# Half-height out matmuls beside the scores, and two gate groups ahead of their value groups

## The chip, the cores and the metric

The kernel runs on one core of a Trainium2 chip. The time is that of the device, in microseconds (us), from start to end of one execution. A time of a kernel is the median of several executions; the profile is of one execution. The engines of the core work from queues of their own: TensorE (PE in the profile, with its weight loads as PEld), VectorE (DVE), ScalarE (ACT), GpSimd (POOL) and the SyncE queue (SP), which here only issues DMAs.

## The reference

Causal attention with 16 extra keys and values ("beacons") that every query may see, for 8 batches of 8 heads with 576 tokens and a head size of 64. Its output, 4608 tokens of 512, goes through a gated feed-forward block with 1536 hidden units.

```
k_all = concatenate([beacon_k, k]);  v_all = concatenate([beacon_v, v])
a = softmax(mask(q @ k_all.T / 8))          # per batch and head
x = (a @ v_all) as 4608 tokens x 512
out = (gelu(x @ w_gate) * (x @ w_val)) @ w_out
```

## The kernel before

One core does everything, batch by batch, and two kinds of work are interleaved: the attention of batch b, and the out projection of chunk b - 1 (a chunk is 512 tokens; there are nine). All engine orders are written out by hand: `keep` holds each instruction in program order on its engine.

**Attention of a batch** (in the loop over `b`). Heads go in four pairs m. The scores of a pair, keys by queries, come in four chunks c of 512, 464, 496 and 208 columns (`CHUNKS`, in the order 0, 2, 1, 3). "Score (m, c)" below is one call part of `scores(b, (m, c))`. Since a head has 64 dimensions, a score matmul uses 64 of the 128 rows of the array; the two heads of a pair use the upper and the lower 64 rows and write to two banks of one buffer. `scores` then has ScalarE take the exp into SBUF (L171), and GpSimd clear the causal triangle (`masks`, L320). `attend` multiplies by the values (`x_ps`), VectorE normalizes (`r_sb`, `y_sb`), and a DMA transpose brings the result to `xT_sb`.

**The feed-forward block of a chunk.** `gate_val(ci, fi)` makes hidden tile fi of twelve: four gate matmuls, four value matmuls (128 rows, 512 columns each), gelu on ScalarE (`ge_sb`), and their product on VectorE (L448, `hT_sb`). `out_mms` makes the out projection, in four token groups ti of twelve matmuls each, summed over fi in one bank, which `out_store` copies to SBUF on VectorE (L467). `o(n)` issues the next n of these 48 matmuls. They lie between the score groups, so that TensorE has work while ScalarE takes exps.

**PSUM.** There are three buffers of two banks (`psum_s`, tag "s"), taken in turn by score groups, by gate/value groups, by some attends and by the transposes of batch 1's last head pair; and two single banks, `psum_t` ("bank t") and `psum_o` ("bank o"), each a pool of one buffer, for out groups (even ti in t, odd ti in o), single-head attends, and transposes. A tile in a pool waits until the readers of the tile that had the buffer before are done.

**The end of a chunk and the start of a batch, before.** Gate/value group 10 takes an "s" buffer. Group 11 is split (`split=True`): its gate goes to bank t, its value to an "s" buffer, so that gelu runs while the value is computed. Then, in batch b, ScalarE loads the table of exp (L593), and TensorE goes: three out matmuls, scores (0,0), (0,2), (0,1), ten out matmuls, scores (0,3)+(1,3), (1,0), (1,2), five out matmuls, the attend of head 0 in bank t, one out matmul, scores (1,1), (2,0), (2,2), the attend of head 1, seven out matmuls, scores (2,1), (2,3)+(3,3), (3,0), and so on. I call the first three score groups the first triple, the next three the second. In batch 1 four transposes of head pair 3 (`transpose_pe`) stand among the ten out matmuls. In chunk 0, the transposes of batch 1's first three head pairs (`transpose_wide`) follow gate/value groups 4, 6 and 8; keys go through bank t and are copied out by VectorE in five copies (L218, L222), queries through bank o and are copied by ScalarE.

Of the kernel before, what the change touches and what calls it, by code (L numbers as in the profile page):

```python
# [7 lines left out]
P = 128  # L8
B, H, S, NB, D = 8, 8, 576, 16, 64
SK = S + NB  # L10
N_TOK = B * S
D_MODEL = 512
D_FF = 1536
F_TILES = D_FF // P
K_CHUNKS = D_MODEL // P
CH = 512
# [24 lines left out]
FP32 = mybir.dt.float32  # L41
BF16 = mybir.dt.bfloat16
ACT = mybir.ActivationFunctionType
ALU = mybir.AluOpType
# [5 lines left out]
def kernel(  # L50
# [12 lines left out]
    nc = tc.nc  # L63
    keep = tc.keep_in_program_order
# [6 lines left out]
    fpool = ctx.enter_context(tc.tile_pool(name="fpool", bufs=3))  # L71
    hpool = ctx.enter_context(tc.tile_pool(name="hpool", bufs=2))
    opool = ctx.enter_context(tc.tile_pool(name="opool", bufs=2))
    psum_s = ctx.enter_context(tc.tile_pool(name="psum_s", bufs=3, space=bass.MemoryType.PSUM))
    psum_t = ctx.enter_context(tc.tile_pool(name="psum_t", bufs=1, space=bass.MemoryType.PSUM))
    psum_o = ctx.enter_context(tc.tile_pool(name="psum_o", bufs=1, space=bass.MemoryType.PSUM))
# [6 lines left out]
    wg_sb = const.tile([P, K_CHUNKS, D_FF], BF16, name="wg_sb", tag="wg_sb")  # L83
    wv_sb = const.tile([P, K_CHUNKS, D_FF], BF16, name="wv_sb", tag="wv_sb")
    wo_sb = const.tile([P, F_TILES, D_MODEL], BF16, name="wo_sb", tag="wo_sb")
    xT_sb = const.tile([P, NPAIR, N_TOK + P - KROWS[4]], BF16, name="xT_sb", tag="xT_sb")
# [80 lines left out]
    def mm(out_ap, lhsT, rhs, start, stop, **kw):  # L167
        keep(nc.tensor.matmul(out_ap, lhsT, rhs, start=start, stop=stop, **kw))  # L168

    def act(out_ap, in_ap, func, **kw):  # L170
        keep(nc.scalar.activation(out_ap, in_ap, func, **kw))  # L171
# [6 lines left out]
    def tr_part(b, m, w, dst):  # L178
        qk, kb = qk6[b]
        for r in range(6):  # L180
            for hi in range(2):
                tr(
                    dst[64 * hi : 64 * hi + 64, r * 96 : (r + 1) * 96],
                    qk[0:96, w, 2 * m + hi, r * D : (r + 1) * D],
                )
        if w:
            tr(dst[:, S:SK], kb[:, 2 * m : 2 * m + 2, :])

    def transpose_pe(b, m, by_act=False):
        t_ps = psum_s.tile([P, 2, 1024], BF16, name="t_ps", tag="s")  # L190
        for w in range(2):
            tr_part(b, m, w, t_ps[:, w, :])
        out_ap = qkT[:, m, :, NB:SK].rearrange("p w (t r) -> p w t r", r=6)
        in_ap = t_ps[:, 0:2, 0:S].rearrange("p w (r t) -> p w t r", r=6)
        keep(nc.vector.tensor_copy(out_ap[:, 1], in_ap[:, 1]))
        if by_act:
            act(out_ap[:, 0], in_ap[:, 0], ACT.Copy)
        else:
            keep(nc.vector.tensor_copy(out_ap[:, 0], in_ap[:, 0]))
        keep(nc.vector.tensor_copy(qkT[:, m, 1, 0:NB], t_ps[:, 1, S:SK]))  # L200
# [208 lines left out]
    h_of, o_of = {}, {}  # L409

    gv_of = {}

    def gv_mms(ci, fi, *kks, split=False, last=False):
        if (ci, fi) not in gv_of:
            if split:
                gv_of[ci, fi] = (
                    psum_t.tile([P, CH], FP32, name="g_ps", tag="t"),
                    psum_s.tile([P, 2, CH], FP32, name="v_ps", tag="s")[:, 0, :],
                )
            else:  # L420
                gv_ps = psum_s.tile([P, 2, CH], FP32, name="gv_ps", tag="s")
                gv_of[ci, fi] = (gv_ps[:, 0, :], gv_ps[:, 1, :])
        n0 = ci * CH

        def part(w):
            for kk in kks:
                mm(
                    gv_of[ci, fi][w],
                    (wg_sb, wv_sb)[w][:, kk, fi * P : (fi + 1) * P],
                    xT_sb[:, kk, n0 : n0 + CH],  # L430
                    kk == 0,
                    last and kk == kks[-1],
                    skip_group_check=True,
                )

        part(0)
        if not split:
            part(1)
        if not last:
            return  # L440
        ge_sb = fpool.tile([P, CH], BF16, name="ge_sb", tag="ge_sb")
        act(ge_sb, gv_of[ci, fi][0], ACT.Gelu)
        if split:
            part(1)
        if ci not in h_of:
            h_of[ci] = hpool.tile([P, F_TILES, CH], BF16, name="hT_sb", tag="hT_sb")
        keep(
            nc.vector.tensor_tensor(  # L448
                out=h_of[ci][:, fi, :], in0=gv_of.pop((ci, fi))[1], in1=ge_sb, op=ALU.mult
            )  # L450
        )

    def gate_val(ci, fi, split=False):
        gv_mms(ci, fi, *range(K_CHUNKS), split=split, last=True)

    def out_mm(ci, ti, fi, o_ps, c0=0, c1=D_MODEL):
        mm(
            o_ps,
            h_of[ci][:, fi, ti * P : (ti + 1) * P],
            wo_sb[:, fi, c0:c1],  # L460
            fi == 0,
            fi == F_TILES - 1,
        )

    def out_store(ci, ti, o_ps, c0=0, c1=D_MODEL):
        o_sb = o_of[ci][0]
        keep(nc.vector.tensor_copy(o_sb[:, ti, c0:c1], o_ps))  # L467
        n0 = ci * CH + ti * P
        stores.append((out[n0 : n0 + P, c0:c1], o_sb[:, ti, c0:c1]))

# [7 lines left out]
    def out_ps(ti):  # L478
        pool, tag = ((psum_t, "t"), (psum_o, "o"))[ti % 2]
        return pool.tile([P, D_MODEL], FP32, name="o_ps", tag=tag)  # L480

    def out_mms(ci, u0, u1):
        for u in range(u0, u1):
            ti, fi = divmod(u, F_TILES)
            if u == 0:
                o_of[ci] = [opool.tile([P, 4, D_MODEL], FP32, name="o_sb", tag="o_sb"), None]
            if fi == 0:
                o_of[ci][1] = out_ps(ti)
            out_mm(ci, ti, fi, o_of[ci][1])
            if fi == F_TILES - 1:  # L490
                out_store(ci, ti, o_of[ci][1])
                if ci >= N_CHUNKS - 2:
                    store(nc.sync)
# [9 lines left out]
            out=eye,  # L503
# [25 lines left out]
    def ahead(n):  # L529
        for load in loads[:n]:  # L530
            load()
        del loads[:n]
# [52 lines left out]
    for b in range(B):  # L585
        u = [0]

        def o(n):
            out_mms(b - 1, u[0], u[0] + n)
            u[0] += n  # L590

        if b:
            keep(nc.scalar.preload_act_table_set(SET_EXP))  # L593
            o(3)
            scores(b, (0, 0))
            scores(b, (0, 2))
            scores(b, (0, 1))
            o(5)
            if b == 1:
                transpose_pe(1, 3)  # L600
            ahead(2)
            o(5)
            scores(b, (0, 3), (1, 3))
            scores(b, (1, 0))
            scores(b, (1, 2))
            ahead(2)
            o(5)
            av_head(b, 0, 0, psum_t, "t")
            o(1)
            scores(b, (1, 1))  # L610
            scores(b, (2, 0))
            scores(b, (2, 2))
            ahead(2)
            av_head(b, 0, 1, psum_t, "t")
            turn_dma(b, 0)
            o(7)
            scores(b, (2, 1))
            scores(b, (2, 3), (3, 3))
            scores(b, (3, 0))
            av_head(b, 1, 0, psum_o, "o")  # L620
            o(5)
            av_head(b, 1, 1, psum_o, "o")
            turn_dma(b, 1)
            scores(b, (3, 1))
            scores(b, (3, 2))
            av(b, 2)
            turn_dma(b, 2)
            o(6)
            av(b, 3)
            turn_dma(b, 3)  # L630
            o(11)
            keep(nc.scalar.preload_act_table_set(SET_GELU))
            for kk in range(K_CHUNKS):
                for fi in range(2):
                    gv_mms(b, fi, kk, last=kk == 3)
        for fi in range(F_TILES):
            if fi >= 2:
                gate_val(b, fi, fi == F_TILES - 1 and b < B - 1)
            if b == 0 and fi in (4, 6, 8):
                transpose_wide(1, (fi - 4) // 2)  # L640
            if fi == 0:
                if b and b + 1 < B:
                    hold(b, 3)
                    load_v(b + 1)
                if b and b + 2 < B:
                    load_qk(b + 2)
                if 2 <= b + 1 < B:
                    transpose_dma(b + 1)
                store(nc.sync)
# [4 lines left out]
    for i, (c0, c1) in enumerate(((0, 384), (384, D_MODEL))):  # L654
        o_ps = out_ps(1 - i)[:, 0 : c1 - c0]
# [34 lines left out]
```

The softmax here doesn't subtract the row's maximum and nothing guards it: scores larger than these inputs give would overflow.

## Time and profile before

| what | value |
|---|---|
| median of 8 runs | 365.69 us (365.13 to 366.11) |
| the profiled execution | 365.64 us, span 363.8 us |
| TensorE busy | 353.6 us (97%), 3092 matmuls recorded |
| ScalarE busy | 193.1 us (53%) |
| VectorE busy | 158.8 us (44%) |
| GpSimd busy | 161.5 us (44%) |
| clock granted to TensorE | 0.999 of full speed |

How to read the lines that follow. A line of the timeline has the start in the span, the duration, the engine, the line of the kernel (L168 is the helper of all matmuls, L171 that of all activations), the operation, the output and inputs by name, how many instructions are merged, and in brackets how long the engine was idle before, and what ended that. A matmul's duration is modelled and overlaps the next one's, so the distances of starts are what counts. A few matmul records are missing in the trace: at 126.18 the timeline has nine out matmuls behind ten weight loads. A line of the waits has the total in us, the number of times and the longest.

### The profile page before, as it was taken

The numbers are of one execution on the slowest core, as the hardware profiler recorded it, in microseconds if no ns is written. First come the engines' busy times: TensorE is split into PE (matmuls) and PEld (weight loads), VectorE is DVE, ScalarE is ACT, GpSimd is POOL, SyncE is SP. The second block draws the span as 40 slices with busy tenths as digits, with TensorE's granted clock in tenths as the row PEclk, the third lists the DMA queues.
The fourth block names the chain that finished last, engine by engine and source line by source line (L and its number), as shares of the span: only waits on it lengthen the run. The fifth ranks groups of instructions, "written<-read, shape, count | busy, mean of one in ns | idle before, by whom it ended". The sixth has DMA issues, their size and how long they took to land.

```text
span 363.8 us, 7576 instructions
## 1 busy us (share of the span) xinstructions
PE 353.6 (97%) x3092; PEld 184.6 (51%) x3134; DVE 158.8 (44%) x314; ACT 193.1 (53%) x252; POOL 161.5 (44%) x288
## 2 busy tenths in 40 slices
PE   7899999999999999999999999999999999999996
PEld 6665446444654455445644464446544554444443
DVE  4557836343443335433534354334444353333332
ACT  3965788237923593349633891369335953321210
POOL 8933397646546562945384555655330530000000
PEclk9999999999999999999999999999999999999999
DMA  7999999899489953999299919991598032000102
GB/s 103 177 204 204 197 124 102 125 135 206 43 125 144 215 48 75 154 216 73 56 150 210 117 40 125 187 183 22 110 139 133 19 65 109 2 0 29 59 34 110
DMA packets 160418, 41.55 MB, mean 114 GB/s; under 512 B 146944, under 2 KB 155904, under 8 KB 160384
## 3 DMA queue, kind: packets, MB, share of 16 engines
q0 software_dynamic: 104848, 19.11, 68.7%
q1 hardware_dynamic: 55536, 21.96, 30.4%
q8 instruction: 24, 0.39, 0.5%
q14 instruction: 10, 0.08, 0.1%
HBM read 38.27 MB, written 9.44 MB: 131 GB/s over the span
## 4 chain that ended last, share of the span: by engine, by line
PE 83%; DMA 8%; POOL 6%; issue 2%; ACT 1%; DVE 0%; POOLq 0%; ACTq 0%
PE gv_ps L168 42%; PE o_ps L168 24%; PE x_ps L168 8%; PE s_ps L168 6%; DMA wo_sb<-in_moe_w_out_dram 5%; DMA qk<-in_q_dram 3%; POOL qk L111 1%; PE v_ps L168 1%; PE g_ps L168 1%; POOL v_sb L111 1%; POOL q_sb L111 1%; POOL wg_sb L111 1%; POOL wv_sb L111 1%; ACT expT L171 1%; POOL expT L320 1%
## 5 line engine op out<-in xcount | busy, mean ns | idle before, releaser
L171 ACT ACTIVATE ge_sb<-gv_ps 128x512 bf16<-128x512 f32 x101 | 59.4, 597 | 141.8 <-PE gv_ps L168 139.5
L448 DVE TENSOR_TENSOR hT_sb<-gv_ps,ge_sb 128x512 bf16<-128x512 f32 x101 | 69.0, 691 | 111.6 <-ACT ge_sb L171 111.5
L168 PE MATMUL gv_ps<-xT_sb,wg_sb 128*128 128x512 bf16 x402 | 111.2, 379 | 0.5
L168 PE MATMUL gv_ps<-xT_sb,wv_sb 128*128 128x512 bf16 x388 | 107.9, 379 | 0.4
L171 ACT ACTIVATE expT<-s_ps 128x992 bf16<-128x992 f32 (+3 forms) x112 | 100.5, 974 | 6.6 <-PE s_ps L168 5.1
L168 PE MATMUL o_ps<-wo_sb,hT_sb 128*128 128x512 bf16 (+2 forms) x420 | 99.9, 373 | 2.0 <-issue 0.9
L320 POOL TENSOR_SCALAR_AFFINE_SELECT expT<-expT 128x256 bf16<-128x256 bf16 (+1 forms) x140 | 52.4, 393 | 47.3 <-ACT expT L171 44.6
L168 PEld LDWEIGHTS <-wv_sb 128*128 128x128 bf16 x432 | 42.3, 98 | 50.6
L168 PEld LDWEIGHTS <-wg_sb 128*128 128x128 bf16 x432 | 42.1, 98 | 49.9
L168 PEld LDWEIGHTS <-hT_sb 128*128 128x128 bf16 x444 | 39.9, 98 | 41.7 <-DVE y_sb L356 1.6
L168 PEld LDWEIGHTS <-expT 128*128 128x128 bf16 (+1 forms) x960 | 33.7, 97 | 10.3 <-DVE y_sb L356 2.9
L467 DVE COPY o_sb<-o_ps 128x512 f32<-128x512 f32 (+2 forms) x37 | 24.9, 672 | 31.3 <-PE o_ps L168 30.2
L168 PE MATMUL x_ps<-v_sb,expT 128*128 128x65 bf16 (+1 forms) x960 | 37.5, 193 | 0.2 <-POOL expT L320 0.2
L111 POOL DMA_DIRECT2D v_sb<-in_v_dram x40 | 33.7, 858 | 6.9 <-DMA wg_sb<-in_moe_w_gate_dram 2.7
L168 PE MATMUL s_ps<-qkT 64*128 64x80 bf16 (+5 forms) x528 | 32.9, 250 | 2.2 <-DVE qkT L239 1.3
L111 POOL DMA_DIRECT2D k_sb<-in_k_dram x30 | 25.2, 843 | 17.5 <-DMA q_sb<-in_q_dram 10.8
L356 DVE TENSOR_TENSOR y_sb<-x_ps,r_sb 128x320 bf16<-128x320 f32 (+1 forms) x47 | 28.8, 612 | 1.6
L111 POOL DMA_DIRECT2D q_sb<-in_q_dram x30 | 25.3, 873 | 8.5 <-DMA v_sb<-in_v_dram 4.7
L354 DVE RECIPROCAL r_sb<-x_ps 128x5 f32<-128x5 f32 (+1 forms) x47 | 9.6, 204 | 42.6 <-PE x_ps L168 42.6
L168 PEld LDWEIGHTS <-qkT 64*128 64x128 bf16 x528 | 17.1, 95 | 17.6 <-issue 12.8
L399 POOL COPY hold_sb<-xT_sb 128x2 bf16<-128x2 bf16 x6 | 1.1, 187 | 30.9 <-DMA xT_sb<-y_sb 30.9
L171 ACT ACTIVATE qkT<-t_ps 64x288 bf16<-64x288 bf16 (+1 forms) x13 | 6.5, 502 | 4.8 <-PE t_ps L176 4.3
(56 smaller groups left out, 127.5 us busy)
## 6 DMA issues: line engine op xcount, KB each, us to landing
out_dram<-o_sb SPq DMA_DIRECT2D x35, 256.0 KB, 7.0
v_sb<-in_v_dram POOLq DMA_DIRECT2D x24, 128.0 KB, 9.5
q_sb<-in_q_dram POOLq DMA_DIRECT2D x18, 128.0 KB, 12.5
k_sb<-in_k_dram POOLq DMA_DIRECT2D x18, 128.0 KB, 5.9
wo_sb<-in_moe_w_out_dram POOLq DMA_DIRECT2D x3, 512.0 KB, 15.4
wg_sb<-in_moe_w_gate_dram POOLq DMA_DIRECT2D x2, 512.0 KB, 11.6
wv_sb<-in_moe_w_val_dram POOLq DMA_DIRECT2D x2, 512.0 KB, 13.3
v_sb<-in_v_dram POOLq DMA_DIRECT2D x8, 112.0 KB, 5.7
```

The costliest lines, as they stand in the source:

```text
L111: keep(nc.gpsimd.dma_start(out=out_ap, in_=in_ap))
L168: keep(nc.tensor.matmul(out_ap, lhsT, rhs, start=start, stop=stop, **kw))
L171: keep(nc.scalar.activation(out_ap, in_ap, func, **kw))
L320: nc.gpsimd.affine_select(out=d, in_=d, pattern=[[0, 2], [1, n]], compare_op=ALU.is_ge, fill=0.0, base=0, channel_multiplier=-1,)
L354: keep(nc.vector.reciprocal(r, x[:, :, :, D:DV]))
L356: nc.vector.tensor_tensor(out=y_of[i][:, :, h0:h1, :].rearrange("p j b d -> p b j d"), in0=x[:, :, :, 0:D], in1=r.to_broadcast([P, h1 - h0 ...
L399: keep(nc.gpsimd.tensor_copy(hold_sb, x[:, 0 : S : S - 1]))
L448: nc.vector.tensor_tensor(out=h_of[ci][:, fi, :], in0=gv_of.pop((ci, fi))[1], in1=ge_sb, op=ALU.mult)
L467: keep(nc.vector.tensor_copy(o_sb[:, ti, c0:c1], o_ps))
```

## The change

Two edits.

First, for batches 2 to 7, the first token group (ti = 0) of the out projection is computed by `out_half_mms`. Each of its twelve steps is two matmuls of 64 rows, the upper and the lower half of the hidden tile; the upper rows' sums (rows 0 to 63) go to bank t, the lower ones' to bank o. At the end VectorE copies the sums in bank o to SBUF, and then adds those in bank t. One of the twelve steps comes ahead of the first triple of scores, eleven between the first and the second triple; six ordinary out matmuls follow the second triple, where there were five. Batch 1 keeps ordinary out matmuls, in the order one, five, (transposes), seven, five.

Second, for every batch but the last, gate/value groups 10 and 11 are computed by `gates_first`: gate 10 into bank t, gate 11 into bank o, each with its gelu, then value 10 and value 11, each in an "s" buffer, each with its product.

```diff
+    def gates_first(ci, *fis):
+        ge_of = {}
+        for fi, (pool, tag) in zip(fis, ((psum_t, "t"), (psum_o, "o"))):
+            g_ps = pool.tile([P, CH], FP32, name="g_ps", tag=tag)
+            part(ci, fi, 0, g_ps)
+            ge_of[fi] = gelu(g_ps)
+        for fi in fis:
+            v_ps = psum_s.tile([P, 2, CH], FP32, name="v_ps", tag="s")[:, 0, :]
+            part(ci, fi, 1, v_ps)
+            gated(ci, fi, v_ps, ge_of[fi])
...
-    def out_store(ci, ti, o_ps, c0=0, c1=D_MODEL):
+    def out_store(ci, ti, o_ps, c0=0, c1=D_MODEL, o_half=None):
         o_sb = o_of[ci][0]
-        keep(nc.vector.tensor_copy(o_sb[:, ti, c0:c1], o_ps))
+        o_ap = o_sb[:, ti, c0:c1]
+        if o_half is None:
+            keep(nc.vector.tensor_copy(o_ap, o_ps))
+        else:
+            keep(nc.vector.tensor_copy(o_ap, o_half))
+            keep(nc.vector.tensor_tensor(out=o_ap, in0=o_ps, in1=o_ap, op=ALU.add))
...
+    def out_half_mms(ci, u0, u1):
+        for fi in range(u0, u1):
+            if fi == 0:
+                o_of[ci] = [opool.tile([P, 4, D_MODEL], FP32, name="o_sb", tag="o_sb"), (out_ps(0), out_ps(1))]
+            halves = o_of[ci][1]
+            for g in range(2):
+                r = slice(64 * g, 64 * g + 64)
+                mm(halves[g], h_of[ci][r, fi, 0:P], wo_sb[r, fi, :],
+                    fi == 0, fi == F_TILES - 1, skip_group_check=True)
+            if fi == F_TILES - 1:
+                out_store(ci, 0, halves[0], o_half=halves[1])
...
         if b:
             keep(nc.scalar.preload_act_table_set(SET_EXP))
-            o(3)
+            o(1, b > 1)
             scores(b, (0, 0))
             scores(b, (0, 2))
             scores(b, (0, 1))
-            o(5)
+            o(5 if b == 1 else 11, b > 1)
             if b == 1:
                 transpose_pe(1, 3)
+                o(7)
             ahead(2)
-            o(5)
             scores(b, (0, 3), (1, 3))
             scores(b, (1, 0))
             scores(b, (1, 2))
             ahead(2)
-            o(5)
+            o(5 if b == 1 else 6)
             av_head(b, 0, 0, psum_t, "t")
...
-            if fi >= 2:
-                gate_val(b, fi, fi == F_TILES - 1 and b < B - 1)
+            if fi >= 2 and (fi < F_TILES - 2 or b == B - 1):
+                gate_val(b, fi)
+            if fi == F_TILES - 2 and b < B - 1:
+                gates_first(b, fi, fi + 1)
```

More of the change, by code (lines that the diff above doesn't have):

```diff
@@ L411, with part @@
     gv_of = {}
[L413 to L422, printed above, removed]
-        n0 = ci * CH
[L425 to L440, printed above, removed]
+    def part(ci, fi, w, ps, kks=range(K_CHUNKS), last=True):
+        n0 = ci * CH
+        for kk in kks:
+            mm(
+                ps,
+                (wg_sb, wv_sb)[w][:, kk, fi * P : (fi + 1) * P],
+                xT_sb[:, kk, n0 : n0 + CH],
+                kk == 0,
+                last and kk == kks[-1],
+                skip_group_check=True,
+            )
@@ L441, in gv_mms, with gelu, gated @@
+    def gelu(g_ps):
         ge_sb = fpool.tile([P, CH], BF16, name="ge_sb", tag="ge_sb")
-        act(ge_sb, gv_of[ci, fi][0], ACT.Gelu)
-        if split:
-            part(1)
+        act(ge_sb, g_ps, ACT.Gelu)
+        return ge_sb
+    def gated(ci, fi, v_ps, ge_sb):
         if ci not in h_of:
             h_of[ci] = hpool.tile([P, F_TILES, CH], BF16, name="hT_sb", tag="hT_sb")
[L447 to L451, printed above, removed]
@@ L453, in gate_val, with gv_mms @@
-    def gate_val(ci, fi, split=False):
-        gv_mms(ci, fi, *range(K_CHUNKS), split=split, last=True)
+        keep(nc.vector.tensor_tensor(out=h_of[ci][:, fi, :], in0=v_ps, in1=ge_sb, op=ALU.mult))
+    def gv_mms(ci, fi, *kks, last=False):
+        if (ci, fi) not in gv_of:
+            gv_of[ci, fi] = psum_s.tile([P, 2, CH], FP32, name="gv_ps", tag="s")
+        gv_ps = gv_of[ci, fi]
+        for w in range(2):
+            part(ci, fi, w, gv_ps[:, w, :], kks, last)
+        if last:
+            gated(ci, fi, gv_ps[:, 1, :], gelu(gv_ps[:, 0, :]))
@@ new lines, in gate_val @@
+    def gate_val(ci, fi):
+        gv_mms(ci, fi, *range(K_CHUNKS), last=True)
+    def gates_first(ci, *fis):
[8 more added lines that the diff above has]
+            gated(ci, fi, v_ps, ge_of[fi])
@@ L480, in out_ps @@
         return pool.tile([P, D_MODEL], FP32, name="o_ps", tag=tag)
+    def out_half_mms(ci, u0, u1):
[5 more added lines that the diff above has]
+                r = slice(64 * g, 64 * g + 64)
+                mm(
+                    halves[g],
+                    h_of[ci][r, fi, 0:P],
+                    wo_sb[r, fi, :],
+                    fi == 0,
+                    fi == F_TILES - 1,
+                    skip_group_check=True,
+                )
+            if fi == F_TILES - 1:
+                out_store(ci, 0, halves[0], o_half=halves[1])
     def out_mms(ci, u0, u1):
@@ L586, with o @@
         u = [0]
-        def o(n):
-            out_mms(b - 1, u[0], u[0] + n)
+        def o(n, halves=False):
+            (out_half_mms if halves else out_mms)(b - 1, u[0], u[0] + n)
             u[0] += n
```

## The prediction

> **What bounds the kernel now.** I read the chain of work that ended last, then the list of waits, then the timeline around the edited places. The profiled execution took 365.64 us, its span 363.8; the sum below is made against these, and the median of the runs (365.69) is the same to 0.05.
>
> ```profile
> PE 83%; DMA 8%; POOL 6%; issue 2%; ACT 1%; DVE 0%; POOLq 0%; ACTq 0%
> ```
>
> And of the waits, all that TensorE's out and score matmuls have on ScalarE or on nothing visible (total, times, longest):
>
> ```profile
> PE o_ps L168 <- issue: 0.9, 6, 0.2
> ...
> PE s_ps L168 <- ACT expT L171: 0.2, 1, 0.2
> ```
>
> TensorE is the chain, and hardly waits. So a wait added to its queue costs its length, unless a later wait shrinks. The start of batch 3 (start, duration, engine):
>
> ```profile
> 123.83 0.81 PE L168 MATMUL v_ps<-xT_sb,wv_sb 128*128 128x512 bf16 x3
> 124.42 1.28 ACT L593 ACT_TABLE_LOAD   x1
> 124.47 0.81 PE L168 MATMUL o_ps<-wo_sb,hT_sb 128*128 128x512 bf16 x3
> 124.75 0.69 DVE L448 TENSOR_TENSOR hT_sb<-v_ps,ge_sb 128x512 bf16<-128x512 f32 x1 [0.48 <-PE v_ps L168]
> 125.22 0.81 PE L168 MATMUL s_ps<-qkT 64*128 64x512 bf16 x14
> ...
> 128.11 0.69 DVE L467 COPY o_sb<-o_ps 128x512 f32<-128x512 f32 x1 [2.67 <-PE o_ps L168]
> 128.22 0.77 PE L168 MATMUL s_ps<-qkT 64*128 64x128 bf16 x14
> 128.68 0.86 ACT L171 ACTIVATE expT<-s_ps 128x832 bf16<-128x832 f32 x1 [0.21 <-PE s_ps L168]
> 128.92 0.61 PE L168 MATMUL o_ps<-wo_sb,hT_sb 128*128 128x512 bf16 x2
> ...
> 130.34 1.93 ACT L171 ACTIVATE expT<-s_ps 128x928 bf16<-128x928 f32 x2
> 131.34 0.11 PEld L168 LDWEIGHTS <-qkT 64*128 64x128 bf16 x3 [0.24 <-issue]
> ```
>
> Out matmuls follow each other at 0.216 (124.47, 124.69). Three end at 125.12, the scores start at 125.22: 0.096 to enter the half-height layout. The second score triple's last pair (80 columns, 0.036) starts at 128.79, the out matmul at 128.92: 0.098 to leave. VectorE starts a product 0.28 after the last value matmul (124.47 to 124.75), and the out copy 0.20 after its group's end (127.90 to 128.11). At 131.34 score (2,2) is 0.12 late, because it needs the buffer of score (1,2), whose exp ends at 131.29.
>
> [...] here the two halves of a score pair start 3 ns apart, and pairs of 512 follow at 0.216 to 0.226. [...] nothing in the trace passes another matmul. [...] the product at 124.75 takes 0.69.
>
> **Part 1: layouts, batches 2 to 7.** Before, TensorE goes full, scores, full, scores, full; after, full, scores with 12 half pairs, full. One leaving and one entering go: -0.194. Twelve pairs replace twelve matmuls at the same 0.216 (pairs of 80 columns follow at 0.035, so a pair of weight loads hides): so I take 0. [...] above, 0.010 each if the 0.226 holds, 0.12 a batch, and rival C if its loads show.
>
> **Part 2: the wait for the third score buffer, batches 1 to 7.** Score (0,1) takes the buffer of the last value group. VectorE frees it at 124.75 + 0.69 = 125.44, plus 0.05 to reach TensorE (below: copy ends at 50.56, load starts at 50.61): 1.02 after the last value matmul. Before, three out matmuls and the other two scores (0.42) bring TensorE there 1.17 after. After, only one out step stands ahead: 0.10 + 0.22 + 0.42 = 0.74. Wait +0.28. Behind it stand the eleven half pairs and all else on TensorE.
>
> **Part 3: the wait for bank o, batches 2 to 7.** The second out group takes the bank of the upper half sums, where before it was free. The half pairs end at 1.02 + 0.215 + 11 x 0.216 = 3.61; the copy out of it starts 0.20 later and lasts 0.69, so TensorE may go at 4.55. It is there at 3.61 + 0.606 (second triple) + 0.098 = 4.31. Wait +0.24; behind it the six out steps and the first attend. The added add, 0.69, ends at 5.2; the attend that wants bank t comes at 5.85 (4.55 + 6 x 0.216), so the second triple and the six out steps hide it; with that cover gone by more than 0.65 it would begin to cost, 0.69 at most.
>
> **Part 4: what ScalarE gives back.** Both gelus now end before the value groups, so the Exp table load is done at about 124.84 and not 125.70; the first exp starts 0.44 earlier. That lead is lost at exp (0,3), which waits for TensorE's second triple (0.21 idle at 128.68 already): it comes 0.13 earlier only. It does suffice, with TensorE later, to remove the 0.12 at 131.34. But score (1,1) now comes 0.31 late, so do the exps from there, while TensorE is then 0.19 late: the buffer of (2,2), free 0.06 before (3,0) wanted it, comes 0.06 late. (Attend, out step and entry bring TensorE to (1,1) after 5.85 + 0.46 + 0.22 + 0.10 = 6.63, against 6.31 before, both after the last value matmul.) Sum of a batch: -0.194 + 0.28 + 0.24 - 0.12 + 0.06 = +0.27, for six batches +1.6. In batch 6 ScalarE stood 0.28 more before exp (0,3) (0.49 idle at 245.60), and TensorE lost it; with half a microsecond of slack there it would be covered: -0.28.
>
> **Part 5: gate 10 of chunk 0.** The end of chunk 0:
>
> ```profile
> 41.08 1.95 DVE L218 COPY qkT<-t_ps 64x288 bf16<-64x288 bf16 x4
> 42.10 1.03 PE L168 MATMUL gv_ps<-xT_sb,wg_sb 128*128 128x512 bf16 x4
> 43.04 0.17 DVE L222 COPY qkT<-t_ps 128x16 bf16<-128x16 bf16 x1
> 43.83 1.03 PE L168 MATMUL g_ps<-xT_sb,wg_sb 128*128 128x512 bf16 x4
> ...
> 50.40 0.16 DVE L200 COPY qkT<-t_ps 128x16 bf16<-128x16 bf16 x1
> 50.61 0.10 PEld L168 LDWEIGHTS <-qkT 64*128 64x128 bf16 x2 [0.27 <-DVE qkT L200]
> ...
> 52.69 0.36 PE L168 MATMUL x_ps<-v_sb,expT 128*128 128x65 bf16 x6 [0.25 <-POOL expT L320]
> ```
>
> The key transposes of the next batch lie in bank t until VectorE's five copies end at 43.21. Before, gate 10 (42.10) used a score buffer, and only gate 11 (43.83) bank t. After, gate 10 wants it at 42.10: 43.21 + 0.05 - 42.10 = +1.17, in front of all. The copies can't start earlier: the product before them ends at 41.16. In batch 1 the wait of part 2 adds 0.28; the wait at 50.61 (0.07) goes, since the transposes there come earlier among the out steps; and the attend's wait for masks at 52.69, really 0.41 by the single records, is absolute (GpSimd queues DMA issues and masks), so it absorbs 0.41. Net +0.97. Other chunks have no transposes there; bank o for gate 11 is free by then (ScalarE's copies end at 42.57).
>
> Moved in SP's and GpSimd's queues: nothing; the order of their instructions is the same, and each store still waits for its own copy. Sum: 0.97 + 1.6 - 0.28 = +2.3. **365.7 + 2.3 = 368.0 us.**
>
> **Rivals.**
> A, the waits shrink: a bank or buffer is free earlier than I have it, or a later wait for ScalarE takes up what batches 2 to 7 lose. Then chunk 0 alone stays, with 0.97 - 0.28: 366.4; with half of the rest, 367.2. For it: each of those terms is a small difference of times near 0.2. Against: VectorE's durations repeat to 0.01.
> B, faster: parts 2 and 3 do not bind, because VectorE gets to the last product and the upper copy 0.3 sooner than I took it. Then each batch gains 0.194 + 0.12, and 0.06 comes back: -0.25 x 6 = -1.5, with -0.28 in batch 6 and +0.97: 364.9. It decides once the two waits together fall under 0.25 a batch and chunk 0's under 1. Against: both start after matmuls by 0.28 and 0.20 wherever the trace has them.
> C, half pairs don't stream: accumulating pairs show one 0.092 load each, 72 x 0.092 = 6.6: 374.6. Against: score pairs hide theirs.
> D, no effect, as though TensorE's waits were all taken up: 365.7. Against: the chain is 83% TensorE.
>
> **How the numbers follow.** Forecast 0.73, own range 367.2 to 369.0 (0.28 of batch 6 recurring, 0.12 a batch for slower pairs, waits down to half). A 0.12, B 0.06, C 0.03, D 0.06. For 8 in 10: 366.6 to 369.1, which takes in most of A. About 0.2%, 0.73 us, is what can be told from no change: faster 0.05, within it 0.09 (D and the lower end of A), slower 0.86.
>
> **What would show it.** After: a TensorE wait on VectorE of 1.2 before the first gate matmul of the pair in chunk 0; each batch a gap of 0.28 before score (0,1) and of 0.24 before the second out group; no drain between the half pairs and the scores; the first exp 0.44 earlier; the wait at score (2,2) gone. The prediction is wrong if half pairs stand over 0.226 apart, if bank t is free at 42.10, or if batches 2 to 7 come out shorter than before.

## The result: 368.49 us, slower by 0.8%, and the profile after

The changed kernel takes 368.49 us in the median (367.65 to 368.72), the kernel before 365.70 in the runs beside it: a ratio of 1.0077, with a 95% interval of 1.0069 to 1.0084. The forecast was 368.0, slower. The profiled execution took 368.24 us, its span is 366.5, which is 2.6 above the span before. The clock granted to TensorE was 1.000 in it, 0.999 before, so the clock is not what differs.

The page's chain, by engine, and of the list of waits the two new ones of TensorE (total, times, longest):

```profile
PE 76%; DMA 10%; POOL 5%; DVE 5%; issue 2%; ACT 1%; DVEq 0%; SPq 0%; POOLq 0%
```

```profile
PE o_ps L168 <- DVE o_sb L473: 1.1, 6, 0.2
PE g_ps L168 <- DVE qkT L222: 1.0, 1, 1.0
```

VectorE, which had 0% of the chain before, now holds 5% of it. Both waits are in the places that were named ahead: six times for the bank of the lower half sums, once for bank t in chunk 0. Here is that one, in the timeline of the changed kernel:

```profile
41.09 1.94 DVE L218 COPY qkT<-t_ps 64x288 bf16<-64x288 bf16 x4
43.04 0.17 DVE L222 COPY qkT<-t_ps 128x16 bf16<-128x16 bf16 x1
43.26 1.41 PEld L168 LDWEIGHTS <-wg_sb 128*128 128x128 bf16 x8 [1.49 <-DVE qkT L222]
43.27 1.90 PE L168 MATMUL g_ps<-xT_sb,wg_sb 128*128 128x512 bf16 x8 [1.00 <-DVE qkT L222]
```

VectorE's copies stand within 0.01 of where they stood before (41.08 and 43.04). The gate matmuls of tile 10 wait for the end of the last, 43.21. The distance from the last value matmul to the first gate matmul is 1.377 in the single records (the trace's record of each matmul, before the timeline merges them), where 0.216 is the pace: 1.16 lost. The bracket says 1.00, because it counts from the modelled end of the last value matmul, 0.379 after its start, and not from 0.216 after it.

The start of batch 3, and the way from the half sums to the second out group:

```profile
125.11 1.28 ACT L618 ACT_TABLE_LOAD   x1
126.11 0.39 PE L168 MATMUL o_ps<-wo_sb,hT_sb 64*128 64x512 bf16 x2
126.29 0.69 DVE L433 TENSOR_TENSOR hT_sb<-v_ps,ge_sb 128x512 bf16<-128x512 f32 x1 [0.17 <-PE v_ps L168]
126.34 1.08 PE L168 MATMUL s_ps<-qkT 64*128 64x512 bf16 x14
126.82 1.02 ACT L171 ACTIVATE expT<-s_ps 128x1024 bf16<-128x1024 f32 x1 [0.43 <-PE s_ps L168]
127.03 0.26 PEld L168 LDWEIGHTS <-qkT 64*128 64x128 bf16 x7 [0.22 <-issue]
127.25 0.39 PE L168 MATMUL o_ps<-wo_sb,hT_sb 64*128 64x512 bf16 x2
...
129.62 0.78 PE L168 MATMUL s_ps<-qkT 64*128 64x128 bf16 x14
129.84 0.69 DVE L473 COPY o_sb<-o_ps 128x512 f32<-128x512 f32 x1 [2.86 <-PE o_ps L168]
130.08 0.86 ACT L171 ACTIVATE expT<-s_ps 128x832 bf16<-128x832 f32 x1 [0.51 <-POOL expT L320]
130.56 0.69 DVE L474 TENSOR_TENSOR o_sb<-o_ps,o_sb 128x512 f32<-128x512 f32 x1
130.58 1.02 PE L168 MATMUL o_ps<-wo_sb,hT_sb 128*128 128x512 bf16 x3 [0.18 <-DVE o_sb L473]
```

The value matmuls end at 126.02 here. Score (0,1) starts at 127.03 (its weight load is the line at 127.03), 0.05 after VectorE ended the product at 126.98; the single records have it 0.28 late, and the eleven half pairs behind it start from 127.25. The list of waits has no line of its own for this wait: the matmuls' modelled ends cover it (the one before starts at 126.72 and ends, as modelled, at 126.92), and among the weight loads it is the 0.22 put down to "issue" at 127.03, one of 57 gaps in one line. Its length is seen in the distance of starts. The second out group starts at 130.58, 0.05 after the copy's end at 130.53: 0.25 beyond the drain, which is what TensorE takes in this trace to go from 64-row to 128-row matmuls (0.09 to 0.10 where it waits for nothing else) or back (0.095, from 126.02 to the half pair at 126.11). The first exp starts 0.80 after the value matmuls, against 1.25 before.

Distances from the end of one chunk's value matmuls to the end of the next (0.216 after the last one's start), from the single records of each trace, in us ("to chunk 0" is from the start of the span, "rest" to its end, with batch 7):

| kernel | median | to chunk 0 | batch 1 | batches 2 to 5, each | batch 6 | rest |
|---|---|---|---|---|---|---|
| before | 365.69 | 45.55 | 40.04 | 38.88 | 39.16 | 83.55 |
| changed | 368.49 | 46.73 | 40.14 | 39.15 | 39.15 | 83.83 |

Chunk 0 loses 1.18, batch 1 0.10, batches 2 to 5 and 7 0.27 or 0.28 each, batch 6 nothing: 2.63 in all, the difference of the spans.

### The profile page after: what moved, and what is told of

Same layout as the page of the kernel before. It is cut to its first block, busy times and chain, and to the rows that moved or that the text cites. A ratio compares the mean times of both kernels' runs of the same rounds, so it can differ in the third digit from the quotient of the medians.

```text
span 366.5 us, 7733 instructions
## 1 busy us (share of the span) xinstructions
PE 354.5 (97%) x3164; PEld 187.2 (51%) x3206; DVE 162.9 (44%) x320; ACT 193.2 (53%) x252; POOL 161.6 (44%) x288
## 4 chain that ended last, share of the span: by engine, by line
PE 76%; DMA 10%; POOL 5%; DVE 5%; issue 2%; ACT 1%; DVEq 0%; SPq 0%; POOLq 0%
PE gv_ps L168 34%; PE o_ps L168 21%; PE x_ps L168 8%; DMA q_sb<-in_q_dram 7%; PE s_ps L168 5%; PE g_ps L168 2%; PE v_ps L168 2%; POOL v_sb L111 2%; DMA k_sb<-in_k_dram 2%; POOL k_sb L111 2%; PE t_ps L176 2%; DMA xT_sb<-y_sb 1%; DVE qkT L235 1%; DVE hT_sb L433 1%; PE w_ps L168 1%
## 5 line engine op out<-in xcount | busy, mean ns | idle before, releaser
L171 ACT ACTIVATE ge_sb<-gv_ps 128x512 bf16<-128x512 f32 x94 | 55.3, 597 | 134.5 <-PE gv_ps L168 132.1
L433 DVE TENSOR_TENSOR hT_sb<-gv_ps,ge_sb 128x512 bf16<-128x512 f32 x94 | 64.2, 691 | 104.6 <-ACT ge_sb L171 102.2
L168 PE MATMUL gv_ps<-xT_sb,wg_sb 128*128 128x512 bf16 x374 | 104.1, 379 | 0.5
L168 PE MATMUL o_ps<-wo_sb,hT_sb 128*128 128x512 bf16 (+3 forms) x492 | 100.8, 373 | 2.6 <-DVE o_sb L473 1.1
L168 PE MATMUL gv_ps<-xT_sb,wv_sb 128*128 128x512 bf16 x360 | 100.7, 379 | 0.4
L168 PEld LDWEIGHTS <-hT_sb 128*128 128x128 bf16 (+1 forms) x516 | 41.3, 96 | 43.5 <-issue 5.2
L168 PE MATMUL s_ps<-qkT 64*128 64x80 bf16 (+5 forms) x528 | 33.7, 250 | 3.1 <-DVE qkT L239 1.6
L471 DVE COPY o_sb<-o_ps 128x512 f32<-128x512 f32 (+2 forms) x31 | 20.7, 668 | 15.2 <-PE o_ps L168 14.1
L168 PEld LDWEIGHTS <-qkT 64*128 64x128 bf16 x528 | 18.8, 95 | 15.8 <-issue 8.1
L433 DVE TENSOR_TENSOR hT_sb<-v_ps,ge_sb 128x512 bf16<-128x512 f32 x14 | 9.7, 692 | 11.5 <-PE v_ps L168 11.5
```

Of the source, the lines that this page charges most:

```text
L433: keep(nc.vector.tensor_tensor(out=h_of[ci][:, fi, :], in0=v_ps, in1=ge_sb, op=ALU.mult))
L471: keep(nc.vector.tensor_copy(o_ap, o_ps))
```

## The experiments

My theory was that three waits for VectorE make the loss: bank t in chunk 0, the third score buffer, and bank o. The rivals were that one of the two edits does it alone, that the waits only move when one of them is taken away, and that half pairs have a cost of their own. Medians of the kernel before beside these runs were 365.61 to 365.67.

**Gates first alone.** Gate groups 10 and 11 first, as in the changed kernel; the out matmuls whole and in the old order:

```diff
-            o(1, b > 1)
+            o(3)
             scores(b, (0, 0))
             scores(b, (0, 2))
             scores(b, (0, 1))
-            o(5 if b == 1 else 11, b > 1)
+            o(5)
             if b == 1:
                 transpose_pe(1, 3)
-                o(7)
             ahead(2)
+            o(5)
...
-            o(5 if b == 1 else 6)
+            o(5)
```

> Gate groups 10 and 11 first, as in the changed kernel, but the out matmuls whole and in the old order (3, 5, 5, 5). My theory: only the wait for bank t in chunk 0 stays, 1.16 before gate 10, of which GpSimd's late masks in batch 1 may absorb up to 0.4; no wait before score (0,1), since three out matmuls stand ahead of the triple again; batches 2 to 7 unchanged at 38.88 each. 366.5 to 366.9. Rival, the half sums are all of the loss: 365.7. Rival, ScalarE's earlier start is worth something by itself: under 366.4, with batches under 38.85.

Measured: 366.58, ratio 1.0035 (1.0015 to 1.0054). To chunk 0 46.71, batch 1 39.83, batches 2 to 5 38.88, batch 6 39.16. The wait in chunk 0 is there again, and nothing else. In batch 3 the scores come no sooner, and the first exp waits for them, no longer for the table:

```profile
124.50 1.28 ACT L618 ACT_TABLE_LOAD   x1
125.41 0.81 PE L168 MATMUL o_ps<-wo_sb,hT_sb 128*128 128x512 bf16 x3
126.16 0.81 PE L168 MATMUL s_ps<-qkT 64*128 64x512 bf16 x14
126.65 1.02 ACT L171 ACTIVATE expT<-s_ps 128x1024 bf16<-128x1024 f32 x1 [0.86 <-PE s_ps L168]
```

The exp stands 1.24 after the value matmuls, as before. So gates first, by itself, buys nothing and costs chunk 0.

**Half sums alone.** Gate/value groups 10 and 11 as before in all chunks, the half pairs as changed:

```diff
+    def gate_split(ci, fi):
+        g_ps = psum_t.tile([P, CH], FP32, name="g_ps", tag="t")
+        v_ps = psum_s.tile([P, 2, CH], FP32, name="v_ps", tag="s")[:, 0, :]
+        part(ci, fi, 0, g_ps)
+        ge_sb = gelu(g_ps)
+        part(ci, fi, 1, v_ps)
+        gated(ci, fi, v_ps, ge_sb)
...
-            if fi >= 2 and (fi < F_TILES - 2 or b == B - 1):
+            if fi >= 2 and (fi < F_TILES - 1 or b == B - 1):
                 gate_val(b, fi)
-            if fi == F_TILES - 2 and b < B - 1:
-                gates_first(b, fi, fi + 1)
+            elif fi == F_TILES - 1:
+                gate_split(b, fi)
```

> The half-height out group and its order, but gate/value group 11 split and group 10 whole as before. My theory: chunk 0 loses nothing; batches 2 to 7 keep both waits (0.28 before score (0,1), 0.24 before the second out group) and come at 39.1 to 39.2 each; the first exp is as late as before. 367.0 to 367.3. Rival, the two parts only cost in company (the early gelus bring the first triple ahead of the product): no wait before score (0,1), batches at 38.9, 365.7.

Measured: 367.12, ratio 1.0044 (1.0029 to 1.0059); batches 39.15 each, to chunk 0 45.28. Score (0,1) is 0.28 late and the second out group 0.21 beyond the drain, much as with both edits. The 0.27 of a batch belongs to the half sums and their order; the early gelus are not what brings the first triple ahead of the product. Neither edit makes the loss alone: against the kernel before, gates first costs 0.91 and the half sums 1.45, both together 2.79 (the 0.43 between is within the parts' intervals).

**Chunk 0 as before.** Only chunk 0 keeps its last two groups; all others as changed:

```diff
-            if fi == F_TILES - 2 and b < B - 1:
+            elif b == 0 and fi == F_TILES - 2:
+                gate_val(b, fi)
+            elif b == 0 and fi == F_TILES - 1:
+                gate_split(b, fi)
+            elif fi == F_TILES - 2:
                 gates_first(b, fi, fi + 1)
```

> The changed kernel, but the last two gate/value groups of chunk 0 as before; all other chunks as changed. My theory: the 1.16 before gate 10 goes and the rest stays: 367.2 to 367.4. Rival, that wait is covered by what batch 1 waits for anyway (GpSimd's masks): 368.1 to 368.5.

Measured: 367.45, ratio 1.0050 (1.0035 to 1.0065). Gate 11 follows at 0.216, to chunk 0 45.64, batches 39.15. It is 0.05 above the range expected. Against the changed kernel's 368.49 it is 1.04 less, a little under the 1.16 of the wait; the rival, that batch 1 covers it, falls. Batch 1 itself takes 40.12 here, without the delay of chunk 0, and 40.14 with it.

**Two half pairs between the scores.** The first triple is spread, without any change of layout:

```diff
             o(1, b > 1)
             scores(b, (0, 0))
             scores(b, (0, 2))
+            if b > 1:
+                o(2, True)
             scores(b, (0, 1))
-            o(5 if b == 1 else 11, b > 1)
+            o(5 if b == 1 else 9, b > 1)
```

> The changed kernel with two of the eleven half pairs moved to stand between scores (0,2) and (0,1), batches 2 to 7; nothing else. My theory: TensorE then comes to score (0,1) after the product is done; the 0.28 goes, nothing takes its place, batches at 38.87, 366.7 to 366.9. Rival, the wait only moves (to the bank of the second out group, or to ScalarE): batches at 39.15, 368.5.

Measured: 366.77, ratio 1.0037 (1.0024 to 1.0050); batches 2 to 5 38.86, batch 6 38.87. The timeline of its batch 3, where the value matmuls end at 125.95:

```profile
126.22 0.69 DVE L433 TENSOR_TENSOR hT_sb<-v_ps,ge_sb 128x512 bf16<-128x512 f32 x1 [0.17 <-PE v_ps L168]
126.27 0.58 PE L168 MATMUL s_ps<-qkT 64*128 64x512 bf16 x6
126.68 0.60 PE L168 MATMUL o_ps<-wo_sb,hT_sb 64*128 64x512 bf16 x4
127.12 0.38 PE L168 MATMUL s_ps<-qkT 64*128 64x80 bf16 x8
...
129.48 0.69 DVE L473 COPY o_sb<-o_ps 128x512 f32<-128x512 f32 x1 [2.57 <-PE o_ps L168]
130.22 0.38 PE L168 MATMUL o_ps<-wo_sb,hT_sb 128*128 128x512 bf16 x1 [0.19 <-DVE o_sb L473]
```

Score (0,1) now starts at 127.12, after the product's end at 126.91, and waits for nothing. The wait for bank o stays as long as it was (0.19 in the bracket, 0.18 in the changed kernel's), so the first wait did not move into the second: the two add up. 0.29 a batch is gone.

**The lower half sums unread.** VectorE copies only bank t; the lower half sums are left out of the first token group's output, so bank o has no reader:

```diff
-            keep(nc.vector.tensor_copy(o_ap, o_half))
-            keep(nc.vector.tensor_tensor(out=o_ap, in0=o_ps, in1=o_ap, op=ALU.add))
+            keep(nc.vector.tensor_copy(o_ap, o_ps))
```

> The changed kernel, but VectorE reads only the upper half sums (bank t); the lower half sums in bank o are left out of the output of the first token group, so nothing holds bank o when the second out group wants it. My theory: the 0.24 before the second out group goes; 0.07 or less comes back at score (3,0), whose buffer waits for exp; batches at 38.9 to 38.98, 367.0 to 367.3. Rival, TensorE's wait there is for something else than the copy, or the attend behind it waits for masks instead: batches at 39.15, 368.5.

Measured: 366.89, ratio 1.0036 (1.0026 to 1.0046), a little better than expected; batches 38.91, batch 6 39.02. The second out group no longer stands behind the copy:

```profile
128.75 0.78 PE L168 MATMUL s_ps<-qkT 64*128 64x128 bf16 x14
128.95 0.69 DVE L473 COPY o_sb<-o_ps 128x512 f32<-128x512 f32 x1 [2.84 <-PE o_ps L168]
129.46 0.82 PE L168 MATMUL o_ps<-wo_sb,hT_sb 128*128 128x512 bf16 x3
```

It starts at 129.46, before the copy's end at 129.64. So it was the copy of the lower sums that held TensorE, for 0.24 a batch.

**The waits mended.** Two half pairs between the scores, chunk 0 as before, and batch 1 in its old order (three, five, transposes, five, five); only the wait for bank o is left:

```diff
-            o(1, b > 1)
-            scores(b, (0, 0))
-            scores(b, (0, 2))
-            scores(b, (0, 1))
-            o(5 if b == 1 else 11, b > 1)
             if b == 1:
+                o(3)
+                scores(b, (0, 0))
+                scores(b, (0, 2))
+                scores(b, (0, 1))
+                o(5)
                 transpose_pe(1, 3)
-                o(7)
-            ahead(2)
+                ahead(2)
+                o(5)
+            else:
+                o(1, True)
+                scores(b, (0, 0))
+                scores(b, (0, 2))
+                o(2, True)
+                scores(b, (0, 1))
+                o(9, True)
+                ahead(2)
             scores(b, (0, 3), (1, 3))
...
```

The lines for chunk 0 are those of the run "Chunk 0 as before".

> Half-height out group in batches 2 to 7 with two half pairs between scores (0,2) and (0,1); chunk 0's last groups as before; batch 1 in its old order. My theory: of the losses only the wait for bank o is left, 0.24 a batch, against 0.19 of drains and 0.12 at score (2,2): batches at 38.85, and batch 6's 0.28 covered: 365.2 to 365.5. Rival, halves cost something more than the waits: 366 and up.

Measured: 365.35, ratio 0.9991 (0.9982 to 1.0000); batches 38.86, batch 6 38.87. That is at the edge of what can be told from the kernel before. One line of its timeline shows what it still pays, six times:

```profile
128.76 0.59 PE L168 MATMUL o_ps<-wo_sb,hT_sb 128*128 128x512 bf16 x2 [0.19 <-DVE o_sb L481]
```

The half pairs thus show no cost beyond the waits.

**The attend two steps sooner.** The version with the waits mended, with four out matmuls instead of six ahead of the first attend, and nine instead of seven behind the second (the lines are set against the changed kernel's):

```diff
-            o(5 if b == 1 else 6)
+            o(5 if b == 1 else 4)
             av_head(b, 0, 0, psum_t, "t")
...
-            o(7)
+            o(7 if b == 1 else 9)
```

> The version before, and two of the six out matmuls ahead of the first attend moved behind the second attend. My theory: ScalarE's exps of the second triple are early enough for the attend to come 0.43 sooner, so that score (1,1) and the exps behind it come 0.4 sooner and the waits of TensorE for ScalarE and GpSimd after it (0.12 and 0.06 in the kernel before) go: batches at 38.75, 364.7 to 365.1. Rival, the attend then waits for the masks of (0,3), and nothing is gained: 365.4.

Measured: 365.66, ratio 0.9998 (0.9989 to 1.0006); batches 38.88 or 38.89, batch 6 39.16. A miss. The attend does come 0.43 sooner and waits for no mask, but score (2,2) then waits 0.09 for the buffer of score (1,2), the wait in the last attend (0.05) stays, and batch 6 shows its 0.28 again:

```profile
129.58 0.91 PE L168 MATMUL s_ps<-qkT 64*128 64x80 bf16 x14
130.12 0.11 PEld L168 LDWEIGHTS <-qkT 64*128 64x128 bf16 x3 [0.21 <-issue]
```

Here it was worth nothing that TensorE reached a score group sooner, because ScalarE had not freed that group's buffer.

**Half sums without gates first, mended.** As the mended version, but the last groups of every chunk as before, and three half pairs ahead of the first triple, nine behind it (parts of the edit, set against the changed kernel):

```diff
-                o(1, True)
+                o(3, True)
                 scores(b, (0, 0))
                 scores(b, (0, 2))
-                o(2, True)
                 scores(b, (0, 1))
                 o(9, True)
...
-            if fi >= 2 and (fi < F_TILES - 2 or b == B - 1):
+            if fi >= 2 and (fi < F_TILES - 1 or b == B - 1):
                 gate_val(b, fi)
...
+            elif fi == F_TILES - 1:
+                gate_split(b, fi)
```

> The version with the waits mended, but without any gate group ahead of its value group: groups 10 and 11 as before in every chunk, and three half pairs ahead of the first triple, nine behind it. The first exp is then as late as before. My theory: ScalarE's earlier start is worth nothing, since its lead was lost at exp (0,3); with three pairs ahead no wait comes at score (0,1), and exp (0,3) can start 0.2 sooner than before, which is enough: batches at 38.86, 365.2 to 365.5. Rival, the earlier start carried the mended version: ScalarE stands in front of TensorE again (0.12 at score (2,2)), batches at 38.98 or more, 366.0 to 366.4.

Measured: 365.70, ratio 1.0000 (0.9993 to 1.0007); batches 38.95. That lies between the two, with the batches nearer to the rival's 38.98. ScalarE starts late, so the buffer of score (0,1) is late when score (1,2) wants it:

```profile
128.53 0.38 PE L168 MATMUL s_ps<-qkT 64*128 64x384 bf16 x4 [0.16 <-ACT expT L171]
128.53 0.11 PEld L168 LDWEIGHTS <-qkT 64*128 64x128 bf16 x3 [0.44 <-issue]
128.84 0.82 PE L168 MATMUL o_ps<-wo_sb,hT_sb 128*128 128x512 bf16 x2
```

By the single records TensorE stands 0.32 there, and then not at all for bank o, since the copy ends meanwhile (at 128.71; the out group starts at 128.84). So once TensorE has lost its waits at the first triple, ScalarE's earlier start is worth 38.95 - 38.86 = 0.09 a batch; the two versions differ too in where two of the half pairs stand, which was not tried apart.

**The mended version with the lower sums unread.** The same edit as above (the lower half sums are left out of the first token group), in the mended version:

```diff
-            keep(nc.vector.tensor_copy(o_ap, o_half))
-            keep(nc.vector.tensor_tensor(out=o_ap, in0=o_ps, in1=o_ap, op=ALU.add))
+            keep(nc.vector.tensor_copy(o_ap, o_ps))
```

> The version with the waits mended, and VectorE does not read the lower half sums, which are left out of the output of the first token group, so that the second out group finds bank o free. What the layout change would be worth with one bank more. My theory: TensorE loses the last added wait, 0.25 a batch: batches at 38.6, 363.6 to 364.1. Rival, ScalarE or GpSimd bound the batch by then and give back half or more: batches at 38.75 or above, 364.7 and up.

Measured: 364.18, ratio 0.9954 (0.9938 to 0.9971); batches 38.62, batch 6 38.73; that is just above the range expected and well under the rival's. The out group follows the scores with nothing but the drain between, 0.70 after the triple's start, as in the kernel before (128.22 to 128.92):

```profile
127.58 0.76 PE L168 MATMUL s_ps<-qkT 64*128 64x128 bf16 x14
128.28 0.82 PE L168 MATMUL o_ps<-wo_sb,hT_sb 128*128 128x512 bf16 x2
```

This is what the two edits together are worth where no bank is short: 38.88 - 38.62 = 0.26 a batch, of which 0.19 are the drains and the rest a wait at score (2,2), less a new one. No run here frees bank o sooner with the lower sums kept.

## Why the prediction was right, and where its size was off

**Part 1, the layouts.** Right. Between the half pairs and the scores no drain is left (in batch 3 the second triple starts 0.216 after the last half pair does), pairs follow at 0.216, and the saving shows in the last run: the drains (0.194) and the wait at score (2,2) (0.12) less 0.07 at score (3,0) make 0.25, and 0.26 was measured.

**Part 2, the third score buffer.** Right. Forecast +0.28; the single records show 0.28, and moving two pairs took away 0.29 a batch.

**Part 3, bank o.** Right. Forecast +0.24; the records show 0.25 beyond the drain, and leaving the lower sums unread took away 0.24. The add of 0.69 was hidden as said (130.56 to 131.25, the attend at 131.87).

**Part 4, what ScalarE gives back.** Right for the changed kernel: first exp 0.44 sooner, exp (0,3) only 0.14 sooner, the wait at score (2,2) gone, 0.07 new at score (3,0). Sum +0.27, measured 0.27. But the early start was not needed for it: with the half sums alone the first exp is as late as before (1.24 after the value matmuls), exp (0,3) still starts 4.06 after them, as in the changed kernel (4.20 before), and the wait at score (2,2) is gone as well. The half sums' order makes the 0.14; the forecast, which credited the wait's end to ScalarE's lead together with TensorE's lateness, had the number without needing the lead. The claim that the lead is lost at exp (0,3) does not carry over to a kernel whose first triple no longer waits: there it is worth some 0.09 a batch, which I had expected to be nothing.

Batch 6's standstill of ScalarE came back in the changed kernel at the same exp and was covered, as forecast (0.79 idle where other batches have 0.51, and the batch no longer than they):

```profile
247.81 2.62 ACT L171 ACTIVATE expT<-s_ps 128x832 bf16<-128x832 f32 x3 [0.79 <-POOL expT L320]
```

It is there in the kernels with gates first alone and with the attend sooner too, where batch 6 has 39.16. What it is was not tried.

**Part 5, chunk 0.** The wait was 1.16; the forecast's own sum, 43.21 + 0.05 - 42.10, is 1.16 too, and stood there as 1.17. The term that was mis-sized is the net with batch 1: +0.97 forecast, 1.18 + 0.10 = 1.28 in the profile. The 0.41 that the first attend had waited for masks was absorbed as I said: up to there the changed kernel is 0.98 late. But GpSimd's masks then cost 0.26 at the attend of pair 2, where they had cost nothing. The first two lines are of the waits between 45 and 62, before and after; the others stand in batch 1 of the changed kernel:

```profile
POOL expT L320 <- ACT expT L171: 0.3, 2, 0.2
POOL expT L320 <- ACT expT L171: 1.4, 3, 0.7
...
58.18 1.62 POOL L111 DMA_DIRECT2D k_sb<-in_k_dram  x2
59.80 2.40 POOL L320 TENSOR_SCALAR_AFFINE_SELECT expT<-expT 128x256 bf16<-128x256 bf16 x7
60.91 0.69 PEld L168 LDWEIGHTS <-expT 128*128 128x128 bf16 x21 [0.21 <-POOL expT L320]
```

GpSimd now waits 1.4 for exps instead of 0.3, and its two DMA issues start at 58.18 where they started at 56.80, and the masks behind them are later too (59.80, before 58.42). The attend of pair 2 waits for one of them; with 0.06 more at a score buffer this makes the 0.3. I had taken the masks' place in GpSimd's queue as given in time, and followed it only as far as the first attend.

The kernel with chunk 0 as before is the closest comparison. The two attends wait 0.24 and 0.03 there, and 0 and 0.26 in the changed kernel: the delay moved the wait and took nothing from it. Yet a wait at the later attend does not need that delay. It is 0.20 with gates first alone, and 0.20 in the mended version, where chunk 0 has no delay and the first attend waits for nothing. What sets GpSimd's place in each trace is not shown.

The other 0.2 between 368.0 and 368.49 is that the median rose by 2.79, the profiled execution by 2.60. The stretch up to the end of chunk 0 also differs by itself, 44.97 to 45.81 in the traces of the seven kernels that don't have the wait there, so tenths of chunk 0 and batch 1 can't be settled from one trace each.

**The rivals.** A, that waits shrink, did not come: batches 2 to 7 lost what was forecast, and batch 1 lost more. B, that the waits of parts 2 and 3 don't bind, fell with the distances in the changed kernel's trace. C, that half pairs don't stream, fell with their pace of 0.216 and with the mended version. D, no effect, fell with the time.

One reading of the profile was incomplete: the list said to hold all waits of out and score matmuls for ScalarE left out a 0.7, once, for the copy of qkT. It lies in the first 45 us and is 0.7 in both kernels, so the sum does not change.

## What to carry to other kernels

Before work is moved ahead on the engine that bounds, ask of each buffer that it reaches sooner who frees it, and when: here a saving of 0.19 in drains was turned into a loss by 0.28 and 0.24 of waiting for a product and a copy on VectorE that took 0.69 each in both kernels. Here two kinds of work share one layout, and their order could be changed without a drain: two half pairs moved between score groups took away a whole wait, 0.29 a batch, and no new one came. Before a delay is counted as absorbed by another late engine, follow that engine's queue to where it is on time again; here the wait came back 7 us later.

## What the runs showed that I had not expected

A wait of 0.28 on TensorE, at each of the seven batch starts, has no line of its own in the list of waits: it is found in the distance between starts (0.315 where 0.036 is the pace, in batches 2 to 7). The two added waits did not overlap (0.28 and 0.24), yet in the half sums without gates first a wait for ScalarE of 0.32 swallowed the wait for bank o whole. The difference is where they stand. The 0.28 lies ahead of the half pairs, and so makes the copy of their sums later by as much (3.82 after the value matmuls, and 3.53 with two half pairs between the scores); the 0.32 lies behind the half pairs, while the copy is already running (from 128.02, and the scores that wait start at 128.53).
